# Second LayerNorm by scaling the first one's turned rows, and MLP chunks in the order 2, 3, 0, 1

## The chip, the cores and the metric

The kernel runs on one core of one Trainium2 chip. The metric is the time of one execution on the device in microseconds (us), as a median of several runs; lower is better.

## What is computed

A transformer block on 2048 tokens of 448 features in float32: a grouped-key attention (16 heads of 28, one key and one value head) and an MLP of 1792 hidden features, both on a normalized input, added to the input. The MLP normalizes a second time:

```python
def _layernorm(x, axis=-1, eps=1e-5):
    m = jnp.mean(x, axis=axis, keepdims=True)
    v = jnp.var(x, axis=axis, keepdims=True)
    return (x - m) / jnp.sqrt(v + eps)

xn = _layernorm(x)
def B(x):                      # the MLP
    y = _layernorm(x)          # the second LayerNorm
    h = gelu_tanh(y @ w1 + b1)
    return h @ w2 + b2
return x + attention(xn) + B(xn)
```

The second LayerNorm of a row has mean zero to start with, so it only multiplies the first one's row by a factor that belongs to the token: 1 / sqrt(v / (v + eps) + eps).

## The kernel before, in words

The 2048 tokens are 16 tiles of 128 tokens, four tiles make a chunk, and there are four chunks. Three stages follow each other.

**QKV.** For each chunk c and each of four column groups i there is a slot (c, i). `q_slot` (line 350) multiplies the turned rows of the chunk with the q, k and v weights; `evac` (360) brings the product from PSUM to SBUF in the next slot and sends q to DRAM (`qd`, 377). While chunk c is multiplied, chunk c + 1 is normalized: `center` (255) computes (x - mean) * rstd for a tile of 128 tokens, ScalarE for 448 columns (263) and VectorE for 64 of them once more (264); `turn` (268) transposes it on TensorE in four 128x128 blocks (272), ScalarE copies the result from PSUM as the high part `xh` (273), and VectorE subtracts for the low part `xl` (274). High and low parts are the two addends in which every factor of a float32 product is kept; a product is three matmuls (high-high, low-high, high-low), in `proj_steps` (175). Features 384 to 447 stand twice in the fourth block, so that it needs only two matmuls. The tiles `xh` and `xl` have two buffers each. During the last chunk, chunk 0 is normalized again with the second norm's factors (`norm_parts` with `second`, called at 447). The factors `lnq` and offsets `lnqb` are made by `norm_both` (231) in slots (2, 2) and (2, 3).

Between the matmuls of the stage the weights of the MLP are loaded and split: `w1_load` and `w1_load2` (315, 320; `pair` is one buffer), `w1_split` (325: ScalarE high, GpSimd low), `w2_load` (332). A dictionary of jobs (`later`, 406) puts small jobs into a given slot. All DMAs of this stage but six are issued by SyncE, in the order of the program: x, weights, the stores `qd<-qe` (377) and `ks<-kl` (374), and the loads of query tiles `qm` and `q3` (`load_m`, 433).

**MLP.** 56 slots, one for each chunk c and each of 14 groups ft of 128 hidden features, in the order of c then ft. `slot` (643) issues `mlp1` (596): 11 matmuls of the first layer into the PSUM tile `ph`, then GELU on ScalarE and GpSimd (lines 603 to 618); and `mlp2` (622) of the slot two before: 12 matmuls of the second layer into four PSUM tiles that are kept for a whole chunk. After each matmul the generator yields, and the main loop (697) puts 9 matmuls of another kind into each slot: score matmuls of the attention (`max_stream`, 511, with a maximum on VectorE at 522, and `turned_scores`, 549, with a scaled copy on VectorE at 556). All of these use the same three PSUM tiles `m`. The twelve places in `mlp2` carry jobs (`stages`): two exponentials of turned scores on ScalarE with their stores to DRAM (`turned_exp`, 568), the second half of w2's split (`low` in `w2_split`, 344, in odd slots of the first chunk), `closing` (high and low part of the GELU, 613), `middle` (tanh and the products after it, 608). In five of fourteen slots of the first three chunks the table `norms` (674) puts `norm_gen` (303) there: it centres and turns the tiles of the next chunk with the second norm's factors, using x rows that `line` (245) has loaded again.

**Attention.** From about 479 us on; the change touches nothing in it.

The order on every engine is the order of the program text (`manual_schedule`); GpSimd, VectorE, ScalarE, TensorE and SyncE's DMA queue each work in order.

Of the kernel before, what the change touches and what calls it, by code (L numbers as in the profile page):

```python
# [16 lines left out]
P = 128  # L17
# [16 lines left out]
LEAD = 11  # L34
NH = 8
# [4 lines left out]
def block_kernel(ctx, tc, x, wq, wk, wv, wo, w1, b1, w2, b2, out):  # L40
# [22 lines left out]
    td = {u: dram.tile([32, 4, 4 * CT, 512], F32, name=f"td{u}") for u in TURNED}  # L63
    qd = [dram.tile([D, S], F32, name=f"qd{i}") for i in range(2)]
# [12 lines left out]
    lnqb = wp.tile([P, NT], F32, name="lnqb")  # L77
# [171 lines left out]
    def norm_parts(c, second, first=False, bank=mtile):  # L249
        xh = xt_p.tile([P, 4, CW], F32R, name="xh")  # L250
        xl = xl_p.tile([P, 4, CW], F32R, name="xl")
        xts[c, second] = xh, xl
        xns = {}

        def center(k):
            t = CT * c + k
            if first:
                xn = f(wqp.tile([P, 2, CW], F32R, name="qe", bufs=5))[:, 0, :]
            else:
                xn = tmp.tile([P, 4 * P], F32, name="xn", bufs=2)  # L260
            scale, bias = (lnq, lnqb) if second else (lnr, lnb)
            src = lines.pop(t) if second and c else xin[t]
            act.activation(xn[:, 0:D], src, AF.Identity, bias=bias[:, t:t + 1], scale=scale[:, t:t + 1])
# [14 lines left out]
    def norm_first(bank):  # L278
        center, turn = norm_parts(0, False, True, bank)
# [72 lines left out]
    def q_slot(c, i):  # L352
        xh, xl = xts[c, False]
# [62 lines left out]
    for k in (2, 3):  # L416
        later(2, k, lambda g=g: next(g))

# [27 lines left out]
    for c in range(NCH):  # L446
        center, turn = norm_parts((c + 1) % NCH, c + 1 == NCH, bank=lambda shape: (qbank, mtile)[next(turns) % 2](shape))
        for i in range(4):
# [22 lines left out]
            for part, k in (("", "c0 c1", "t0 c2 t1 c3", "t2 t3") if c == 0 else  # L471
                            ("c0 c1", "t0 c2 t1 c3", "t2 t3", ""))[i].split():
                (center if part == "c" else turn)(int(k))
# [122 lines left out]
    def mlp1(c, ft):  # L596
        yh, yl = xts[c, True]
# [24 lines left out]
    def mlp2(c, ft, stages):  # L622
# [8 lines left out]
        for n, (k, i) in enumerate(order):  # L631
# [3 lines left out]
            if ft == NF - 1 and i == 2:  # L635
                t = CT * c + k
# [6 lines left out]
    def slot(n):  # L643
# [17 lines left out]
        if n in norms:  # L661
            stages = {4: norms[n], 5: texp, 6: texp, 7: closing, 8: norms[n], 9: middle, 10: low}
# [9 lines left out]
    norms, maxed, ending, later_low = {}, 0, none, none  # L672
    mslots = [(c, ft) for c in range(NCH) for ft in range(NF)]
    for c in range(1, NCH):
        g = norm_gen(c, lambda shape: php.tile(shape, F32, name="ph"))
        for i in range(CT + 1):
            norms[NF * (c - 1) + 5 + 2 * i] = lambda g=g: next(g, None)
    mxs.add(max_stream())
    done = 0
    for n in range(len(mslots) + 2):  # L680
        c, ft = mslots[n] if n < len(mslots) else (NCH, n - len(mslots))
        if 3 <= ft < 11 and ft % 2 and c < NCH - 1:
            line(CT * (c + 1) + (ft - 3) // 2)
        if 9 < ft:
            line(CT * c + ft - 10)
            if ft > 10:
                a = lines[CT * c + ft - 11]
                pool.tensor_add(a, a, b2b)
        if ft == 0 and n:
            a = lines[CT * c - 1]  # L690
# [263 lines left out]
```

## Time and profile before

| | us |
|---|---|
| median of 3 runs (lowest to highest) | 1092.6 (1092.5 to 1093.32) |
| profiled execution | 1092.67 |
| its span in the trace | 1090.9 |
| QKV stage, to the first MLP matmul | 66.2 |
| MLP stage | about 412 |
| attention | about 612 |

In the rows of the trace a line like `start us, us, engine, line, operation, out<-in xcount` is one instruction or a run of equal ones. PE is TensorE, DVE is VectorE, ACT is ScalarE, POOL is GpSimd and SP is SyncE. A bracket at the end tells how long the engine was idle before it and what ended that. Groups of instructions have their count, busy time and the mean of one in ns. In rows of stretches the columns are the stretch, its length, each engine's busy time with a count, the granted clock of TensorE, the busy share of the DMA engines and GB/s. Lines are those of the kernel before.

### The profile page before, as it was taken

The numbers are of one execution on the slowest core, as the hardware profiler recorded it, in microseconds if no ns is written. First come the engines' busy times: TensorE is split into PE (matmuls) and PEld (weight loads), VectorE is DVE, ScalarE is ACT, GpSimd is POOL, SyncE is SP. The second block draws the span as 40 slices with busy tenths as digits, with TensorE's granted clock in tenths as the row PEclk, the third lists the DMA queues.
The fourth block names the chain that finished last, engine by engine and source line by source line (L and its number), as shares of the span: only waits on it lengthen the run. The fifth ranks groups of instructions, "written<-read, shape, count | busy, mean of one in ns | idle before, by whom it ended". The sixth has DMA issues, their size and how long they took to land.

```text
span 1090.9 us, 17542 instructions
## 1 busy us (share of the span) xinstructions
PE 1079.5 (99%) x5777; PEld 713.7 (65%) x5777; DVE 910.4 (83%) x1847; ACT 736.4 (68%) x1279; POOL 562.5 (52%) x694
## 2 busy tenths in 40 slices
PE   9999999999999999999999999999999999999998
PEld 8778888888888888865555556555556455555444
DVE  7789889888988998887898997899986889876744
ACT  6675565666666666559777776677775777765783
POOL 6359787778767877854343433433342343243220
PEclk9999999999999999999999999999999999999999
DMA  8774555777877777767977799588797778895720
GB/s 274 214 231 136 154 145 157 194 176 185 217 181 180 183 201 180 214 161 156 200 189 175 183 212 214 141 198 193 183 202 183 175 172 194 203 197 137 183 46 35
DMA packets 140512, 195.15 MB, mean 179 GB/s; under 512 B 17086, under 2 KB 96116, under 8 KB 140420
## 3 DMA queue, kind: packets, MB, share of 16 engines
q1 hardware_dynamic: 127684, 172.11, 63.0%
q0 software_dynamic: 11328, 21.33, 8.9%
q8 instruction: 46, 0.75, 0.3%
q10 hardware_dynamic: 1408, 0.57, 0.2%
q14 instruction: 46, 0.38, 0.1%
HBM read 115.22 MB, written 77.71 MB: 177 GB/s over the span
## 4 chain that ended last, share of the span: by engine, by line
PE 89%; ACT 3%; DVE 3%; DMA 2%; POOL 1%; issue 1%; SPq 0%; DVEq 0%; ACTq 0%; POOLq 0%
PE po L840 22%; PE m L521 17%; PE m L871 17%; PE m L633 10%; PE ph L180 9%; PE m L555 5%; PE qp L180 1%; DMA td<-raw 1%; PE m L752 1%; DVE mx L522 1%; PE m L753 1%; PE m L754 1%; PE ph L185 1%; PE ph L183 1%; ACT raw L573 1%; PE m L399 1%
## 5 line engine op out<-in xcount | busy, mean ns | idle before, releaser
L522 DVE TENSOR_REDUCE mx<-m 128x1 f32<-128x512 f32 x784 | 506.5, 680 | 81.1 <-PE m L521 72.3
L872 ACT ACTIVATE p<-m 128x512 f32<-128x512 f32 x784 | 402.6, 609 | 163.2 <-PE m L871 163.2
L521 PE MATMUL m<-ks,qm 128*128 128x512 f32 x784 | 322.1, 411 | 0.1
L871 PE MATMUL m<-xh,ks 128*128 128x512 f32 x784 | 258.6, 399 | 1.0 <-DVE half L723 1.0
L840 PE MATMUL po<-p,vs 128*32 128x512 f32 x2048 | 246.0, 598 | 0.0
L521 PEld LDWEIGHTS m<-ks,qm 128*128 128x128 f32 x784 | 147.0, 187 | 117.9 <-ACT p L872 34.5
L871 PEld LDWEIGHTS m<-xh,ks 128*128 128x128 f32 x784 | 144.2, 188 | 52.0 <-ACT p L872 15.0
L556 DVE TENSOR_SCALAR_CACHE_REDUCE raw<-m 128x512 f32<-128x512 f32 x240 | 161.1, 689 | 15.2 <-PE m L555 7.0
L854 DVE STREAM_TRANSPOSE p<-half 128x1024 f32<-128x1024 f32 x120 | 148.2, 1236 | 5.3 <-PE po L840 3.3
L573 ACT ACTIVATE raw<-raw,m 128x1024 f32<-128x1024 f32 x120 | 133.1, 1151 | 0.0
L840 PEld LDWEIGHTS po<-p,vs 128*32 128x32 f32 x2048 | 53.5, 109 | 120.1 <-issue 114.2
L603 ACT ACTIVATE hx<-ph,b1t 128x512 f32<-128x512 f32 x55 | 37.9, 690 | 131.9 <-PE ph L185 122.1
L555 PE MATMUL m<-ks,q 128*128 128x512 f32 x240 | 94.8, 395 | 1.1 <-DVE mx L522 0.6
L618 POOL TENSOR_TENSOR hl<-hx,hh 128x512 fp32r<-128x512 f32 x56 | 73.2, 1306 | 34.6 <-ACT hh L616 34.6
L633 PE MATMUL m<-w2h,hl 128*128 128x448 f32 x224 | 82.5, 370 | 0.3 <-POOL hl L618 0.3
L633 PE MATMUL m<-w2l,hh 128*128 128x448 f32 x224 | 81.4, 365 | 0.4 <-DVE w2l L346 0.4
L633 PE MATMUL m<-w2h,hh 128*128 128x448 f32 x224 | 81.4, 364 | 0.1
L611 POOL TENSOR_TENSOR hx<-hx,hz 128x512 f32<-128x512 f32 x56 | 73.1, 1306 | 4.7
L606 POOL TENSOR_TENSOR hz<-hz,hx 128x512 f32<-128x512 f32 x56 | 72.8, 1299 | 4.7
L508 POOL DMA_DIRECT2D xh<-mn x15 | 8.1, 543 | 124.3 <-ACT mn L504 124.3
L180 PE MATMUL ph<-xh,w1h 128*128 128x512 f32 x165 | 65.0, 394 | 0.0
L180 PE MATMUL ph<-xh,w1l 128*128 128x512 f32 x165 | 64.6, 391 | 0.0
(181 smaller groups left out, 1376.0 us busy)
## 6 DMA issues: line engine op xcount, KB each, us to landing
td<-raw SPq DMA_DIRECT2D x240, 256.0 KB
half<-td SPq DMA_DIRECT2D x120, 512.0 KB
xh<-qd POOLq DMA_DIRECT2D x60, 168.0 KB, 4.6
a<-in_A_x_dram SPq DMA_DIRECT2D x32, 224.0 KB
qm<-qd POOLq DMA_DIRECT2D x112, 56.0 KB, 4.4
qd<-qe SPq DMA_DIRECT2D x24, 256.0 KB
qm<-qd SPq DMA_DIRECT2D x84, 56.0 KB
ad<-a SPq DMA_DIRECT2D x16, 224.0 KB
```

What stands on the lines that cost most here:

```text
L180: pe.matmul(ps, w, v, start=(n == 0), stop=False)
L521: pe.matmul(pm, qm[:, t * P:(t + 1) * P], ks[:, n * CW:(n + 1) * CW], start=True, stop=True)
L522: dve.tensor_reduce(mx[:, CT * j + t, n:n + 1], pm, axis=AX.X, op=ALU.max)
L555: pe.matmul(sc, q3[i][:, t * P:(t + 1) * P], ks[:, n * CW:(n + 1) * CW], start=True, stop=True)
L556: dve.tensor_scalar(raw[:, :, 4 * n:4 * n + 4, :].rearrange("p r b i -> p b r i"), sc.rearrange("p (b r i) -> p b r i", r=4, i=32), SCALE, ...
L573: act.activation(raw[:, rs], raw[:, rs], AF.Exp, bias=m3[:, 4:5], scale=1.0)
L618: pool.tensor_sub(hl, hx, f(hh))
L633: pe.matmul(m2[k], h[:, k * P:(k + 1) * P], w[:, ft, :], start=(ft == 0 and i == 0), stop=(ft == NF - 1 and i == 2))
L840: pe.matmul(po[32 * j:32 * j + 32, :], vs[:, kt, :], ps.pop((u, kt, j)), start=(kt == 0), stop=(kt == NT - 1))
L854: dve.transpose(p.rearrange("p k (g j) -> p g k j", j=32), halves[u, kt // 8][:, :, 32 * (kt % 8):32 * (kt % 8) + 64].rearrange("p g (k j) ...
L871: pe.matmul(s, ks[:, kt * P:(kt + 1) * P], qss[u][:, j, :], start=True, stop=True)
L872: act.activation(p, s, AF.Exp, scale=SCALE)
```

## The change

The second norm no longer starts from x. The turned rows of the first norm are taken, high and low part are added again (`join`), multiplied with a tile that holds the factors of the chunk's 512 tokens in every partition (`scaled`), and split again (`high` on ScalarE, `low` on VectorE), block by block of 128 features. The factors are transposed once on TensorE (`scale_rows`), written to DRAM, and read back as a broadcast row for each chunk (`scale_load`). Chunks 2 and 3 are still in SBUF at the end of QKV and are scaled in place; chunks 0 and 1 are joined during QKV by GpSimd, stored to DRAM (`put`) and read back in the MLP (`take`). So the MLP takes the chunks in the order 2, 3, 0, 1. Chunk 2 is scaled in the last two QKV slots, with products on VectorE; the others in the MLP, with products on GpSimd, and for chunk 3 the join on VectorE. `norm_both` runs one slot earlier, and the centred tiles of the first norm are kept in the GELU's buffers `hz`.

```diff
+MLP_ORDER = 2, 3, 0, 1
...
+    xd = [dram.tile([P, 4, CW], F32, name=f"xd{c}") for c in range(2)]
+    sd = dram.tile([NCH, CW], F32, name="sd")
...
-        dve.tensor_mul(lnq, lnq, lnr)
-        dve.scalar_tensor_tensor(lnqb, lnp[:, :, 0], -1.0, lnq, op0=ALU.mult, op1=ALU.mult)
...
-                xn = tmp.tile([P, 4 * P], F32, name="xn", bufs=2)
-            scale, bias = (lnq, lnqb) if second else (lnr, lnb)
-            src = lines.pop(t) if second and c else xin[t]
+                xn = hrp.tile([P, CW], F32, name="hz", bufs=2)
+            scale, bias, src = lnr, lnb, xin[t]
...
-    def norm_gen(c, bank):
-        center, turn = norm_parts(c, True, False, bank)
-        for k in range(CT + 1):
-            if k > 0:
-                turn(k - 1)
-            yield
-            if k < CT:
-                center(k)
-            yield
+    scales, parts = {}, {}
+
+    def scale_rows():
+        pa = mtile([NT, P])
+        pe.transpose(pa, lnq, ident)
+        at = part_tile()[0:NT, 0:P]
+        dve.tensor_copy(at, pa)
+        nc.sync.dma_start(sd.rearrange("c (k p) -> (c k) p", p=P), at)
+
+    def scale_load(c):
+        scales[c] = tmp.tile([P, CW], F32, name="ab", bufs=1)
+        nc.sync.dma_start(scales[c], sd[c:c + 1, :].to_broadcast([P, CW]))
+
+    def part_tile():
+        return tmp.tile([P, CW], F32, name="part", bufs=1)
+
+    def join(c, b, eng, part):
+        xh, xl = xts[c]
+        parts[c, b] = part
+        eng.tensor_add(part, f(xh[:, b, :]), f(xl[:, b, :]))
+
+    def put(c, b):
+        n = P if b < 3 else 64
+        nc.sync.dma_start(xd[c][0:n, b, :], parts.pop((c, b))[0:n])
+
+    def take(c, b):
+        n = P if b < 3 else 64
+        parts[c, b] = part_tile()
+        for r in range(0, P, n):
+            nc.sync.dma_start(parts[c, b][r:r + n], xd[c][0:n, b, :])
+
+    def scaled(c, b, eng):
+        eng.tensor_mul(parts[c, b], parts[c, b], scales[c])
+
+    def high(c, b):
+        if c < 2 and b == 0:
+            xts[c] = xt_p.tile([P, 4, CW], F32R, name="xh"), xl_p.tile([P, 4, CW], F32R, name="xl")
+        act.activation(xts[c][0][:, b, :], parts[c, b], AF.Copy)
+
+    def low(c, b):
+        yh, yl = xts[c]
+        dve.tensor_sub(yl[:, b, :], parts.pop((c, b)), f(yh[:, b, :]))
...
-    for k in (2, 3):
+    for k in (1, 2):
         later(2, k, lambda g=g: next(g))
+    later(2, 3, scale_rows)
+    later(2, 3, lambda: scale_load(2))
+    for c in range(3):
+        for b in range(4):
+            name = "hz" if c == 2 and b > 1 else "hx"
+            later(c, b, lambda c=c, b=b, name=name: join(c, b, pool, hrp.tile([P, CW], F32, name=name, bufs=2)))
+            if c < 2:
+                later(c + (b + 1) // 4, (b + 1) % 4, lambda c=c, b=b: put(c, b))
+    for b in range(4):
+        later(3, 2, lambda b=b: scaled(2, b, dve), b < 2)
+        later(3, 2, lambda b=b: high(2, b), b < 2)
+    for b in range(4):
+        later(3, 2 + b // 2, lambda b=b: low(2, b), b > 1)
...
-        if n in norms:
-            stages = {4: norms[n], 5: texp, 6: texp, 7: closing, 8: norms[n], 9: middle, 10: low}
+        stages.update(seconds.pop(n, {}))
...
+    for i, c in enumerate(MLP_ORDER[1:]):
+        for b in range(4):
+            n = NF * i + 4 + 2 * b
+            seconds[n] = {11: lambda c=c, b=b: scaled(c, b, pool)}
+            if c > 1:
+                seconds[n][6] = lambda c=c, b=b: join(c, b, dve, part_tile())
+            seconds[n + 1] = {7: lambda c=c, b=b: high(c, b), 11: lambda c=c, b=b: low(c, b)}
...
-        if 3 <= ft < 11 and ft % 2 and c < NCH - 1:
-            line(CT * (c + 1) + (ft - 3) // 2)
+        if ft == 1 and c < NCH - 1:
+            scale_load(MLP_ORDER[c + 1])
+        if 4 <= ft < 12 and ft % 2 == 0 and c < NCH - 1 and MLP_ORDER[c + 1] < 2:
+            take(MLP_ORDER[c + 1], ft // 2 - 2)
```

What is left out renames tiles by `MLP_ORDER[c]` where it was c, drops the fourth call of `norm_parts` in QKV, and drops `lnqb`.

More of the change, by code (lines that the diff above doesn't have):

```diff
@@ L247, in line, with norm_parts @@
         nc.sync.dma_start(lines[t], xv[:, t, :])
-    def norm_parts(c, second, first=False, bank=mtile):
+    def norm_parts(c, first=False, bank=mtile):
         xh = xt_p.tile([P, 4, CW], F32R, name="xh")
         xl = xl_p.tile([P, 4, CW], F32R, name="xl")
-        xts[c, second] = xh, xl
+        xts[c] = xh, xl
         xns = {}
@@ L352, in q_slot @@
     def q_slot(c, i):
[L353 removed]
+        xh, xl = xts[c]
         cols = slice(c * CW, (c + 1) * CW)
@@ L670, in none @@
         pass
-    norms, maxed, ending, later_low = {}, 0, none, none
+    maxed, ending, later_low = 0, none, none
     mslots = [(c, ft) for c in range(NCH) for ft in range(NF)]
[L674 to L677, printed above, removed]
+    seconds = {}
+    for i, c in enumerate(MLP_ORDER[1:]):
[5 more added lines that the diff above has]
+            seconds[n + 1] = {7: lambda c=c, b=b: high(c, b), 11: lambda c=c, b=b: low(c, b)}
     mxs.add(max_stream())
```

18 lines of the change are left out of this document (9 added, 9 removed).

## Prediction

> **What bounds the kernel now.** I read the page first, then TensorE's rows in order of time, and then the queues that must feed the changed part: SyncE's DMA issues, VectorE, ScalarE and GpSimd around one MLP slot.
>
> ```profile
> span 1090.9 us, 17542 instructions
> ...
> PE 89%; ACT 3%; DVE 3%; DMA 2%; POOL 1%; issue 1%; SPq 0%; DVEq 0%; ACTq 0%; POOLq 0%
> ```
>
> The chain is TensorE for 89%. The profiled execution took 1092.67 us (1.8 us beside its span), the median is 1092.6, so a difference in the trace is a difference of the median. A measurement of this kernel can tell about 0.2%, 2.2 us, from no change.
>
> The changed part lies in the QKV stage (to 66.24 us) and the MLP (56 slots, to about 479). In the MLP TensorE streams with no gap. The last first-layer matmul (L185) of a slot shows the slot's length; here those of slots 6, 7 and 8, and of 21 and 22:
>
> ```profile
> 106.63 0.39 PE L185 MATMUL ph<-xl,w1h 128*128 128x512 f32 x1
> 113.66 0.39 PE L185 MATMUL ph<-xl,w1h 128*128 128x512 f32 x1
> 121.77 0.39 PE L185 MATMUL ph<-xl,w1h 128*128 128x512 f32 x1
> ...
> 216.24 0.39 PE L185 MATMUL ph<-xl,w1h 128*128 128x512 f32 x1
> 223.87 0.39 PE L185 MATMUL ph<-xl,w1h 128*128 128x512 f32 x1
> ```
>
> A plain slot is 7.03 us. One that turns a tile for the second norm is 7.63, or 8.11 where VectorE also splits w2. Three turns have the 8.11 and nine about 7.63. So the second norm costs the MLP 3 x 1.08 + 9 x 0.60 = 8.6 us now.
>
> **What goes.** All 64 transposes of the second norm: 48 in the MLP, worth those 8.6 us, and 16 in the last QKV chunk:
>
> ```profile
> 58.58 0.60 PE L272 MATMUL qp<-ident,xn 128*128 128x128 f32 x4
> 59.02 0.60 PE L272 MATMUL m<-ident,xn 128*128 128x128 f32 x4
> ...
> 62.43 0.65 PE L272 MATMUL qp<-ident,xn 128*128 128x128 f32 x4
> 63.21 0.66 PE L272 MATMUL m<-ident,xn 128*128 128x128 f32 x4
> ...
> 66.47 0.39 PE L180 MATMUL ph<-xl,w1h 128*128 128x512 f32 x1
> ```
>
> They hold TensorE from 58.58 to 59.37 and from 62.43 to 63.63, 2.0 us. The one new transpose (the factors, 16x128) costs as much as a quarter of a row of four, 0.1. By itself this would end QKV 1.9 us earlier. The x rows that were read again for three chunks are replaced by as many bytes (eight parts of 256 KB and four broadcasts). I cost that exchange at nothing: the DMA share in the MLP (last column but one) leaves room, and a part has a whole slot until GpSimd wants it. If a part came later than that, GpSimd's product and what follows it would be late by the same.
>
> ```profile
> 66.24:478.70 412.46, 409.36 (x1859) 341.63 (x1858) 369.63 (x811) 253.88 (x357) 320.21 (x308) 1.00 0.68 177
> ```
>
> Also gone are ScalarE's and VectorE's halves of the second norm, 16 times centring and 16 times splitting a turned tile:
>
> ```profile
> L263 ACT ACTIVATE xn<-a,lnqb,lnq 128x448 f32<-128x448 f32 x12 | 9.0, 752 | 0.0
> L274 DVE TENSOR_TENSOR xl<-ph,xh 128x512 fp32r<-128x512 f32 x12 | 8.3, 692 | 11.3 <-ACT xh L273 11.3
> ```
>
> I count nothing for them: they stand beside TensorE's stream, and the slots of 8.11, where they don't, are counted already. The statistics of the second norm move one QKV slot ahead (some 1 us of small VectorE work in front of evictions); the wait found below covers that.
>
> **What comes in the MLP.** Twelve subtractions ("low") on VectorE, each behind a ScalarE copy ("high"), which stands behind the slot's tanh; twelve products on GpSimd; four sums ("join") on VectorE. GpSimd has room for its products: it is busy for 320 of the 412 us above, and twelve at L618's 1.3 are 16. The low does not fit. One slot begins at 198.96:
>
> ```profile
> 198.87 0.62 ACT L616 ACTIVATE hh<-hx 128x512 fp32r<-128x512 f32 x1
> 199.39 0.62 ACT L609 ACTIVATE hz<-hz 128x512 f32<-128x512 f32 x1
> ```
> ```profile
> 199.57 1.30 POOL L618 TENSOR_TENSOR hl<-hx,hh 128x512 fp32r<-128x512 f32 x1 [0.58 <-ACT hh L616]
> ```
> ```profile
> 199.70 0.69 DVE L556 TENSOR_SCALAR_CACHE_REDUCE raw<-m 128x512 f32<-128x512 f32 x1
> ```
> ```profile
> 201.72 0.39 PE L555 MATMUL m<-ks,q 128*128 128x512 f32 x1
> ```
>
> VectorE reaches the low when it would take the L556 of 199.70. But the high starts behind the tanh (L609), 0.52 later as these two follow each other, and takes 0.62 like L616: 199.91 to 200.53. Then GpSimd's L618 runs until 200.87. A VectorE subtraction of two SBUF tiles does not run beside a GpSimd tensor operation, as the w2 splits show:
>
> ```profile
> 164.03 0.65 DVE L346 TENSOR_TENSOR w2l<-raw,w2h 128x448 fp32r<-128x448 f32 x1
> ```
> ```profile
> 86.67 1.48 DVE L346 TENSOR_TENSOR w2l<-raw,w2h 128x448 fp32r<-128x448 f32 x1
> ```
> ```profile
> 86.37 1.30 POOL L611 TENSOR_TENSOR hx<-hx,hz 128x512 f32<-128x512 f32 x1
> ```
>
> The slow one started 1.0 us before L611's end and waited it out. So the low works from 200.87 to about 201.4. The delayed L556 frees its PSUM bank at 201.4 + 0.69 = 202.1. The scores have three banks; the fourth score matmul is the one of 201.72, and it waits 0.4 us. A low costs 0.45 with the hiccup behind a stall. Without the port wait it would be 0.2, and where it meets a w2 split, 0.75. I take 0.45. Slot 15, where four adds of 0.61 delay VectorE, shows the mechanism:
>
> ```profile
> 179.75 0.68 DVE L556 TENSOR_SCALAR_CACHE_REDUCE raw<-m 128x512 f32<-128x512 f32 x1
> ```
> ```profile
> 180.50 0.50 PE L555 MATMUL m<-ks,q 128*128 128x512 f32 x1
> ```
>
> The first bank was free at 179.75 + 0.68 = 180.43, and the fourth score starts at 180.50, 0.07 behind that. Sum: 12 x 0.45 + 4 joins x 0.1 = 5.8. **MLP: 8.6 + 0.3 (one more stall at a transpose) - 5.8 = 3.1 us gained**, bounds 0 and 6.
>
> **What comes in QKV, and decides.** Chunk 2 is now first in the MLP, and its rows must be multiplied by the broadcast factors first. These go to DRAM and back, issued by SyncE behind the loads of the second q3 tile. SyncE runs late:
>
> ```profile
> 39.33 1.85 SPq L438 DMA_DIRECT2D qm<-qd  x4
> ```
> ```profile
> 43.23 0.44 SPq L100 DMA_DIRECT2D pair<-in_B_w_dram  x1
> ```
> ```profile
> 60.01 2.91 SPq L438 DMA_DIRECT2D q<-qd  x4
> ```
>
> The q<-qd loads are issued two slots ahead of the transposes of 58.58 in the program, but leave after them, until 62.9. So the factors' write leaves at 62.9 at the earliest, however early VectorE has them. The same pattern is in the trace, a small write to DRAM and its broadcast back:
>
> ```profile
> tr<-ld POOLq DMA_DIRECT2D x56, 64.0 KB, 3.6
> ```
> ```profile
> ld<-rc POOLq DMA_DIRECT2D x14, 8.0 KB, 3.9
> ```
>
> That is 3.9 + 3.6 = 7.5 us (bounds 4 and 11, as these are of GpSimd's queue at another time), and SyncE stands still for the first part. The factors are there at 70.4 if nothing else is late.
>
> The Trainium skill (page "DMA: Bandwidth & Descriptors", section "Anatomy of one DMA") has a fixed cost of about 2.0 us and 436 GB/s above it for a transfer from another queue, which would be an estimate of 4.6 us for the two. By it the sum below would be 2.9 us less.
>
> More is late. SyncE must also issue eight new stores ("put"). GpSimd's joins share two buffers with them, so a join waits for the store two before it to land, and w1's splits wait behind that join:
>
> ```profile
> 39.44 1.65 POOL L329 TENSOR_TENSOR w1l<-pair,w1h 128x672 fp32r<-128x672 f32 x1 [2.65 <-ACT w1h L328]
> 41.17 0.67 POOL L330 TENSOR_TENSOR w1h<-pair,w1h 64x224 fp32r<-64x224 f32 x1
> ```
> ```profile
> SPq L377 <- DMA pair<-in_B_w_dram: 3.5, 2, 2.2
> ```
>
> This split (the fourth) releases the load of 43.23. In the new order join (1,2) stands ahead of it and waits for put (1,0). SyncE issues that behind the qm loads, at 41.2, and by the 3.6 above it lands at 44.8; join 1.3 and split 2.3 make 48.4, so the load leaves 5.2 us later and SyncE stands idle before it. It gets back up to 2.2, its longest wait for the landing of such a load, as the queue has drained meanwhile. The factors' write leaves 3.0 late, at 65.9 (bounds 0, if the stores land at once, and 8, if the other stores and joins add theirs in full). The factors land at 73.4.
>
> Then VectorE does four products and the first low, 5 x 0.65 = 3.2, before TensorE's second MLP matmul: 76.6, where it is 66.47 now, +10.1. Behind them stand two more lows and two PSUM evictions ahead of the first score bank, so the fourth score of slot 0 waits too: +1 (0 to 2). **QKV: 11.1 us lost**, the 2 us of transposes being swallowed by the wait. TensorE's queue is in order; nothing behind can fill it. The attention is not touched: its work is the same and comes later.
>
> **Sum:** 11.1 - 3.1 = +8.0 us; 1092.6 + 8.0 = 1100.6. Own range 1095 (no store delays) to 1106.
>
> **Rivals.**
> *The factors come in time* (faster). Place: the write and broadcast of the factors. If they land by 62, TensorE goes from QKV into the MLP 2.0 us earlier than now: 1092.6 - 2.0 - 3.1 = 1087.5. It turns at a landing near 66.3, where the loss equals the 3.1 of the MLP. For it: the factors are worked out a slot earlier than they were. Against: the 62.9 of SyncE, which nothing in the change advances. 0.14.
> *About even:* no store delays (write at 62.9) and lows near 0.2, a gain of 5.8 in the MLP; with 7.5 for the two transfers that is 11.1 - 3.0 - 5.8 = +2.3, and a microsecond less for them, as SyncE's may be quicker than GpSimd's, puts it inside 2.2. 0.08.
> *The joins hold the turns.* The turned tiles have two buffers, so chunk 2's turns wait for join (0,3), chunk 3's for join (1,3), which wait for stores. By my times they are let go about 1 us late; if each store lands 3 us later, TensorE waits in both chunks and the chain above moves by some 5: 1105.6. 0.15.
> *A cold TensorE.* At the start of the trace the same 128x128 matmuls come at 20 in 4.0 us, and then 23 in 2.4:
>
> ```profile
> 1.70:5.70 4.00, 4.00 (x20) 4.00 (x20) 1.00 0.99 281
> 5.80:8.20 2.40, 2.40 (x23) 2.40 (x22) 1.00 1.09 374
> ```
>
> That is 0.20 against 0.104, so the first 20 lost 1.9 us. If the wait before the MLP brings this back, 1102.5. The Trainium skill ("TensorE: Matmul & The Clock Gate", "What's actually happening") says an idle window of about 3.4 us halves the clock until one such window was busy. The trace agrees for the start; no stretch of it is idle that long later, so it can't show the rest. Slot 0 waits for VectorE as well, which would hide part. 0.12.
>
> **How the numbers follow.** Forecast 0.51, with the two slower rivals 0.78 slower by over 0.2%; same 0.08; faster 0.14. Range 1092 to 1108: from the edge of "even" to the joins' case with 2.4 us for a later store.
>
> **What would show it.** TensorE idle for about 10 us before the first MLP matmul, released by ScalarE's high or VectorE's low, and these by the broadcast; SyncE's factor write near 66; no L272 after the third chunk; MLP slots of 7.03 throughout, but for about 7.5 with a low. I am wrong if the broadcast lands before 66, if lows cost over 0.7, or if the gap before the MLP is there and the end comes no later.

## The result and the profile after

The changed kernel takes 1113.17 us as a median (1112.05 to 1115.53, five runs), the kernel before 1092.6 us (1092.31 to 1093.32, five runs): the ratio is 1.0188, 95% interval 1.0177 to 1.02. The forecast was 1100.6 us, in a range of 1092 to 1108. The profiled execution took 1112.07 us, 19.4 us more than that of before.

Two rows of TensorE's timeline cut that difference into stages: the last first-layer matmul of MLP slot 1 and that of slot 55 (columns: start, duration, engine, line, operation). It is L185 before and L187 after. First before, then after.

```profile
72.85 0.39 PE L185 MATMUL m<-xl,w1h 128*128 128x512 f32 x1
461.83 0.39 PE L185 MATMUL ph<-xl,w1h 128*128 128x512 f32 x1
```
```profile
87.51 0.40 PE L187 MATMUL m<-xl,w1h 128*128 128x512 f32 x1
481.55 0.39 PE L187 MATMUL ph<-xl,w1h 128*128 128x512 f32 x1
```

| stage | before | after | difference | forecast |
|---|---|---|---|---|
| to the end of MLP slot 1 | 72.85 | 87.51 | +14.7 | +11.1 |
| MLP slots 2 to 55 | 388.98 | 394.04 | +5.1 | -3.1 |
| from there to the end of the span | 629.07 | 628.55 | -0.5 | 0 |

The rest, 0.2 us, lies outside the span. So both stages came out worse than forecast, and the MLP with the other sign.

**QKV.** SyncE's timeline after shows the two dependent transfers: the write of the factors, and the broadcast load that waits for it.

```profile
66.13 1.83 SPq L483 DMA_DIRECT2D q<-qd  x4
68.06 0.31 SPq L309 DMA_DIRECT2D sd<-part  x1
72.01 0.34 SPq L313 DMA_DIRECT2D ab<-sd  x1
```

The write leaves right behind the query loads, at 68.06, where 65.9 was forecast. VectorE's timeline shows the load's end, four products and the first of the subtractions:

```profile
75.68 1.29 DVE L334 TENSOR_TENSOR hx<-hx,ab 128x512 f32<-128x512 f32 x2 [5.07 <-DMA ab<-sd]
76.89 1.28 DVE L334 TENSOR_TENSOR hz<-hz,ab 128x512 f32<-128x512 f32 x2
78.10 1.28 DVE L343 TENSOR_TENSOR xl<-hx,xh 128x512 fp32r<-128x512 f32 x2
```

From 68.06 to 75.68 are 7.6 us (7.5 were forecast). TensorE's first and second MLP matmul wait for what comes of it; the bracket is the idle time and what ended it:

```profile
77.09 0.80 PE L182 MATMUL ph<-xh,w1h 128*128 128x512 f32 x1 [4.93 <-ACT xh L339]
78.83 0.80 PE L182 MATMUL ph<-xl,w1h 128*128 128x512 f32 x1 [0.95 <-DVE xl L343]
```

The second is at 78.83; it was at 66.47 before. TensorE's own stream is late too. Its waits from 20 to 84 us, grouped by what it waited for (us in total, times, longest):

```profile
PE ph L182 <- ACT xh L339: 4.9, 1, 4.9
PE qp L271 <- ACT hz L262: 3.6, 4, 2.1
PE m L306 <- DVE lnq L203: 1.9, 1, 1.9
PE ph L182 <- DVE xl L343: 0.9, 1, 0.9
PE m L271 <- DVE hz L263: 0.9, 1, 0.9
```

The L271 rows are the turns of chunks 2 and 3 that wait for their centred tiles (5.5 us with two smaller groups that are not shown), and L306 is the factors' transposition. The longest wait, 2.1 us, is ahead of chunk 3's turns. Before the centring VectorE works out chunk 3's statistics, on four columns. Two of these steps take 1.26 and 1.52 us where the two ahead of them (at 46.01 and 46.21) take 0.16 and 0.17, and each ends with an instruction of GpSimd, first a join and then a split of w1. First VectorE, then GpSimd:

```profile
46.41 1.26 DVE L203 SCALAR_TENSOR_TENSOR lnr<-rs 128x4 f32<-128x4 f32 x1
47.70 1.52 DVE L222 SCALAR_TENSOR_TENSOR lnb<-lnp,lnr 128x4 f32<-128x4 f32 x1
```
```profile
46.33 1.32 POOL L321 TENSOR_TENSOR hx<-xh,xl 128x512 f32<-128x512 f32 x1 [4.21 <-DMA xd<-hx]
47.60 1.60 POOL L361 TENSOR_TENSOR w1l<-pair,w1h 128x672 fp32r<-128x672 f32 x1
```

By its bracket the join had itself waited 4.21 us for a store to land.

**MLP.** A plain slot is longer than before: from 205.81 to 212.89 are 7.08 us.

```profile
205.81 0.39 PE L185 MATMUL ph<-xh,w1h 128*128 128x512 f32 x1
212.89 0.39 PE L185 MATMUL ph<-xh,w1h 128*128 128x512 f32 x1
```

The mean over long stretches is 7.07, before it was 7.03. And the slot behind a low of chunk 3 is 8.2 to 8.3 us, behind the last of the four 9.3. Behind the lows of chunks 0 and 1 it is 7.51, behind the last of each four 8.57. Here is one of chunk 3, first ScalarE, then VectorE, then TensorE:

```profile
118.83 0.63 ACT L655 ACTIVATE hz<-hz 128x512 f32<-128x512 f32 x1 [1.81 <-POOL hz L652]
119.37 0.62 ACT L339 ACTIVATE xh<-part 128x512 fp32r<-128x512 f32 x1
```
```profile
120.09 1.62 DVE L343 TENSOR_TENSOR xl<-part,xh 128x512 fp32r<-128x512 f32 x1 [0.75 <-ACT xh L339]
```
```profile
122.38 0.51 PE L601 MATMUL m<-ks,q 128*128 128x512 f32 x1 [0.86 <-DVE raw L602]
```

The rounding (L339, "high") stands behind the tanh (L655), and the tanh waits for GpSimd, whose chain carries the product with the factors and a w2 split as well. So VectorE stands still at its subtraction (L343, "low"), 0.75 us by this row, with the score evictions behind it, and TensorE's score waits for a bank. All twelve lows together:

```profile
L343 DVE TENSOR_TENSOR xl<-part,xh 128x512 fp32r<-128x512 f32 x12 | 13.4, 1114 | 13.5 <-ACT xh L339 10.1 <-POOL hl L664 3.4
```

VectorE was busy with them for 13.4 us and idle ahead of them for 13.5.

### The profile page after: what moved, and what is told of

It is laid out like the page before. It is cut to its first block, busy times and chain, and to the rows that moved or that the text cites. A ratio compares the mean times of both kernels' runs of the same rounds, so it can differ in the third digit from the quotient of the medians.

```text
span 1110.1 us, 17459 instructions
## 1 busy us (share of the span) xinstructions
PE 1079.5 (97%) x5714; PEld 708.6 (64%) x5714; DVE 922.7 (83%) x1838; ACT 726.0 (65%) x1263; POOL 596.7 (54%) x718
## 4 chain that ended last, share of the span: by engine, by line
PE 80%; ACT 5%; DVE 4%; DMA 4%; issue 2%; POOL 2%; SPq 2%; DVEq 0%; ACTq 0%; POOLq 0%
PE po L891 21%; PE m L922 17%; PE m L567 17%; PE m L679 9%; PE ph L182 7%; PE m L601 4%; DMA td<-raw 2%; ACT raw L619 2%; PE m L803 1%; SPq L483 1%; PE m L804 1%; PE m L805 1%; DVE raw L602 1%; PE ph L187 1%; PE ph L185 1%
## 5 line engine op out<-in xcount | busy, mean ns | idle before, releaser
L568 DVE TENSOR_REDUCE mx<-m 128x1 f32<-128x512 f32 x784 | 502.8, 678 | 79.1 <-PE m L567 74.6
L182 PE MATMUL ph<-xh,w1h 128*128 128x512 f32 x165 | 65.9, 400 | 4.9 <-ACT xh L339 4.9
L182 PE MATMUL ph<-xl,w1h 128*128 128x512 f32 x165 | 66.3, 402 | 0.9 <-DVE xl L343 0.9
```

The source lines that it names most:

```text
L182: pe.matmul(ps, w, v, start=(n == 0), stop=False)
L568: dve.tensor_reduce(mx[:, CT * j + t, n:n + 1], pm, axis=AX.X, op=ALU.max)
```

## The experiments

The theory after these rows: four separate losses, (1) the factors' way through SyncE and DRAM, (2) joins and stores that hold SyncE and the turns, (3) the low's wait for the high, (4) the longer plain slot. Rivals: a cold TensorE, and VectorE having no room for the lows at all. "Slot 1 ends" is the time of the row shown above for each kernel's profiled execution. In some of these executions a single MLP slot had a stall of some 1.5 us more, which moves a single profile, not the medians. The kernel before ran beside each set of experiments, with medians of 1092.97 to 1093.3 us, and the ratios are against those; by the ratios the gains over the changed kernel come out up to 0.8 us larger than by the times.

| kernel | time (lowest to highest) | ratio to before, interval | slot 1 ends | slots 2 to 55 |
|---|---|---|---|---|
| before | 1092.6 | | 72.85 | 388.98 |
| changed | 1113.17 (1112.05-1115.53) | 1.0188, 1.0177-1.02 | 87.51 | 394.04 |
| a1_place | 1112.78 (1111.93-1115.9) | 1.0184, 1.0169-1.0199 | 89.25 | 395.94 |
| a2_no_puts | 1106.53 (1105.55-1108.47) | 1.0124, 1.0109-1.0139 | 81.24 | 394.00 |
| a3_known_factors | 1109.03 (1108.93-1110.24) | 1.0147, 1.0132-1.0162 | 83.28 | 394.29 |
| a4_high_early | 1106.01 (1105.48-1107.07) | 1.0115, 1.0098-1.0132 | 89.11 | 387.28 |
| b1_warm | 1121.13 (1116.45-1123.4) | 1.0239, 1.022-1.0258 | 97.22 | 395.61 |
| b2_joins_only | 1108.98 (1108.37-1112.44) | 1.0148, 1.0134-1.0162 | 84.77 | 396.91 |
| b3_before_w1_moved | 1095.86 (1095.62-1097.74) | 1.0027, 1.0018-1.0036 | 73.31 | 391.49 |
| b4_early_factors | 1100.26 (1099.44-1103.48) | 1.0068, 1.0054-1.0081 | 85.66 | 383.96 |
| c1_two_chunks | 1096.38 (1095.95-1097.59) | 1.0033, 1.002-1.0045 | 80.17 | 385.11 |
| c2_stores_by_gpsimd | 1101.25 (1100.01-1101.73) | 1.0073, 1.0059-1.0086 | 86.29 | 384.41 |
| d1_two_chunks_order | 1093.5 (1093.19-1094.59) | 1.0006, 0.9997-1.0014 | 76.61 | 386.09 |
| d2_all_order | 1098.1 (1097.56-1098.62) | 1.0046, 1.003-1.0061 | 84.46 | 383.71 |
| e1_products_shared | 1093.48 (1092.33-1094.91) | 1.0005, 0.9996-1.0014 | 76.73 | 386.40 |
| e2_lows_later | 1094.72 (1092.73-1095.83) | 1.0012, 1.0003-1.0021 | 77.57 | 386.32 |

### The longer plain slot: where the weights lie

The change removes the 64-byte tile `lnqb`, and all that is allocated behind it moves down by 64 bytes. In a1 an unused tile takes its place; in b3 the kernel *before* gets the same shift for w1h and w1l (and three small tiles) alone.

```diff
+    gap = wp.tile([P, NT], F32, name="gap")
     b1t = wp.tile([P, NF], F32, name="b1t")
```
```diff
-    lnqb = wp.tile([P, NT], F32, name="lnqb")
     b1t = wp.tile([P, NF], F32, name="b1t")
...
     w1l = wp.tile([P, 3, F], F32R, name="w1l")
+    lnqb = wp.tile([P, NT], F32, name="lnqb")
```

> The changed kernel with one more small tile of 64 bytes a partition, never used, in the place of the removed one, so that the weights w1h and w1l, the tiles of hrp and w2h and w2l lie at the addresses they had before. If the slower plain MLP slot (7.07 us instead of 7.03 us) comes from where the operands lie, a plain slot is 7.03 us again and the kernel takes 2.3 us less (55 slots x 0.041): about 1110.9 us. If it comes from the order of the instructions or from the engines beside TensorE, the slot stays at 7.07 us and the time at 1113.2 us.

> The kernel before, with its 64-byte tile lnqb allocated behind w1l instead of ahead of b1t, so that w1h and w1l alone lie 64 bytes lower, as in the changed kernel, and nothing else differs. If the place of w1 makes a plain slot 7.07 us, this kernel takes 2.3 us more than before: 1094.9 us. If it is the place of w2h, w2l or the tiles of hrp, or no matter of places, it takes as long as before: 1092.6 to 1093.3 us.

Two neighbouring slot ends in a1, and two in b3:

```profile
209.15 0.39 PE L186 MATMUL ph<-xh,w1h 128*128 128x512 f32 x1
216.18 0.39 PE L186 MATMUL ph<-xh,w1h 128*128 128x512 f32 x1
```
```profile
196.68 0.40 PE L185 MATMUL ph<-xl,w1h 128*128 128x512 f32 x1
203.78 0.40 PE L185 MATMUL ph<-xl,w1h 128*128 128x512 f32 x1
```

In a1 a plain slot is 7.03 us again; in b3 it is 7.07 to 7.11 us. The time of a1 doesn't settle it (0.4 us less where 2.3 were expected; its interval is 3 us wide, and the profiled execution, the longest of its four, had two of the stalls named above), but b3's does: 2.9 us more than before (interval 2.0 to 3.9) from moving tiles by 64 bytes, with the order of the instructions unchanged. In the trace it is a few ns on a matmul: from 270 to 300 us the means of the first layer's groups are 389 to 394 ns before and 393 to 399 ns in b3. Why these addresses are slower, no run here shows.

### Factors, joins and stores

a2 leaves out joins and stores of chunks 0 and 1 (first diff), b2 the stores alone (second diff, with the same loads of w1's rows in the MLP). a3 reads chunk 2's "factors" from a row of w1, early (third diff).

```diff
-    for c in range(3):
+    for c in range(2, 3):
         for b in range(4):
...
-            nc.sync.dma_start(parts[c, b][r:r + n], xd[c][0:n, b, :])
+            nc.sync.dma_start(parts[c, b][r:r + n], w1[0:n, 320 * b:320 * b + CW])
```
```diff
-            if c < 2:
-                later(c + (b + 1) // 4, (b + 1) % 4, lambda c=c, b=b: put(c, b))
```
```diff
-    later(2, 3, lambda: scale_load(2))
+    def known(c):
+        scales[c] = tmp.tile([P, CW], F32, name="ab", bufs=1)
+        nc.sync.dma_start(scales[c], w1[c:c + 1, 0:CW].to_broadcast([P, CW]))
+
+    later(2, 0, lambda: known(2))
```

> Leaves out the joins and the stores to DRAM of chunks 0 and 1; the loads in the MLP read rows of w1 instead, so chunks 0 and 1 of the MLP work on other numbers at the same cost. If the stores hold SyncE and the joins hold the turns (TensorE waits of 1.17 us at 33.08 and 2.22 us at 50.13, the pair load of w1 at 49.97 instead of 43.23), the QKV part ends 3 to 5 us earlier, the factors' write leaves SyncE at 63 to 65 instead of 68.06, and the kernel takes 3 to 5 us less: about 1109. If the write is late for its own reasons (the wait of 2.09 us for lnq ahead of the transposition at 60.85, the queue's other loads), less than 1 us is gained: 1112 to 1113.

> Leaves out the stores of chunks 0 and 1 to DRAM, but keeps GpSimd's joins (the MLP's loads read rows of w1 again, so chunks 0 and 1 work on other numbers). Without joins and stores the kernel took 1106.5 us. If the stores are what delays QKV, through SyncE's queue, this takes 1106.5 to 1108 us. If it is the joins, which hold xh and xl and VectorE's small operations (one of the 16-column steps of lnq took 0.17 us or up to 1.5 us), it stays at 1111 to 1113 us.

> Chunk 2's factors are read from a row of w1 early in its slot 0 instead of from the stored factors, so that nothing waits for the write and the load behind it; chunk 2 is scaled by wrong numbers, all instructions stay. If the two transfers make the wait between QKV and MLP and that idle time makes TensorE cold, the second MLP matmul follows the last QKV matmul (near 72) at once, slot 0 runs at full clock, and the kernel takes 6 to 8.5 us less: 1105 to 1107. If VectorE's own backlog (products and lows behind the rest of its queue) is what is late, at most 2 us is gained: 1111 or more. Without the cold clock in it, 5 us: 1108.

The write of the factors leaves SyncE at 62.19 in a2 and at 65.02 in b2, 68.06 in the changed kernel; a2's row, then b2's:

```profile
62.19 0.31 SPq L309 DMA_DIRECT2D sd<-part  x1
```
```profile
65.02 0.31 SPq L309 DMA_DIRECT2D sd<-part  x1
```

So the joins alone make the write 2.8 us later and the stores another 3.0. In time, the stores are worth 4.2 us and the joins 2.4 (1113.17, 1108.98, 1106.53). The turns' waits of 5.5 us are 1.2 us in a2. Both halves of the theory hold, neither alone: a2 was expected at about 1109 and went lower, b2 lies between its two cases.

a3 gained 4.1 us, less than the 6 to 8.5 expected, and nearest to the 5 that it gave without a cold clock: without the wait for the factors TensorE's own QKV stream, which the turns make late, is the next bound. Its first MLP matmul follows the last QKV matmul at once:

```profile
72.69 0.40 PE L187 MATMUL qp<-xl,wah 128*128 128x512 f32 x1
72.92 0.44 PE L182 MATMUL ph<-xh,w1h 128*128 128x512 f32 x1
74.61 0.50 PE L182 MATMUL ph<-xl,w1h 128*128 128x512 f32 x1 [1.24 <-DVE xl L343]
```

**The cold TensorE** did come. Two stretches of slots 0 and 1 of the changed kernel (the figure after the five busy times is the granted clock):

```profile
79.40:83.24 3.84, 3.84 (x10) 3.01 (x9) 3.84 (x5) 1.25 (x2) 2.82 (x2) 0.50 0.69 253
84.00:87.05 3.05, 3.05 (x15) 2.49 (x14) 3.02 (x10) 2.37 (x4) 1.35 (x2) 1.00 0.23 86
```

By a3 it cost nothing. From the second MLP matmul to the end of slot 1 the changed kernel takes 87.51 - 78.83 = 8.68 us; a3, which is not cold (a granted clock of 1.00 from 74.6 to 83.3), takes 83.28 - 74.61 = 8.67 us. a3 waits for VectorE instead: its third and fourth low and the evictions behind them set the end. Before, the same stretch took 72.85 - 66.47 = 6.38 us.

b1 was to test this by idle matmuls that keep TensorE busy:

```diff
     evac()
+    spin(50, mtile([P, P]))
     ph1a.close()
```

> The changed kernel with 50 idle matmuls of 128 columns (0.09 us each by the transposes' rows, 4.5 us) between the last QKV matmul and the MLP, so that TensorE does not stand idle while the factors come. If slot 0's slow matmuls (0.43 us instead of 0.23 us) cost the 2.2 us that slot 0 is longer by, the kernel takes about 2 us less: 1111. If the next wait takes their place (with the factors known early slot 0 ended 6.25 us earlier but slot 1 waited 1.95 us more), less than 0.5 us is gained: 1112.7 to 1113.2. In an execution whose QKV stream ends only at 77 the idle matmuls come on top, up to 4 us.

The experiment missed. The 50 matmuls left 100 records and held TensorE from 79.39 to 90.47, 11.1 us instead of the 4.5 expected, and QKV ended late in this execution anyway (the wait for `lnq` was 5.3 us, not 1.9). It says nothing on the cold clock; a3 against the changed kernel does.

### The low waits for the high

```diff
-            seconds[n + 1] = {7: lambda c=c, b=b: high(c, b), 11: lambda c=c, b=b: low(c, b)}
+            seconds[n + 1] = {4: lambda c=c, b=b: high(c, b), 11: lambda c=c, b=b: low(c, b)}
```

> The second norm's rounding on ScalarE goes from stage 7 to stage 4 of its slot, ahead of the tanh that waits for GpSimd; nothing else changes. If VectorE's wait for that rounding (0.75 to 1.1 us for each of chunk 3's four lows, 2.27 us for the last of chunks 0 and 1) is what the MLP loses, that goes and the kernel takes 5 to 8 us less: 1105 to 1108. If the lows cost because VectorE has no room for 0.7 to 1.6 us more of work, the stalls of TensorE stay at 1.0 us a low in chunk 3's stage and the time within 1 us: 1112 to 1113.

One digit, and 7.2 us: 1106.01. The same slot as above on ScalarE, now with the rounding ahead of the tanh, and the slot behind the low on TensorE:

```profile
118.49 0.63 ACT L339 ACTIVATE xh<-part 128x512 fp32r<-128x512 f32 x1
120.42 0.63 ACT L655 ACTIVATE hz<-hz 128x512 f32<-128x512 f32 x1 [1.29 <-POOL hz L652]
```
```profile
116.10 0.39 PE L185 MATMUL ph<-xh,w1h 128*128 128x512 f32 x1
123.17 0.40 PE L185 MATMUL ph<-xh,w1h 128*128 128x512 f32 x1
```

The slot of 8.2 us is 7.07 us long. VectorE's group of the lows after that edit:

```profile
L343 DVE TENSOR_TENSOR xl<-part,xh 128x512 fp32r<-128x512 f32 x12 | 16.8, 1396 | 3.1 <-ACT xh L339 2.7 <-DMA q<-qd 0.4
```

The idle time ahead of the lows fell from 13.5 to 3.1 us, though each got longer (1396 ns; it now begins while GpSimd works). So it was the wait; the rival that VectorE has no room falls for chunk 3's lows. In the other two stages the lows of blocks 0 to 2 still cost the 0.44 us of before the edit, slots of 7.51 against 7.07, and the last ones 0.9 (slots of 8.0) instead of 1.5.

### The mends together, and a version with two chunks

b4 joins the unused tile, the early high, and chunk 2's factors worked out early from its own four tiles. c2 is b4 with the stores issued by GpSimd. c1 keeps the factors for chunks 2 and 3 alone and turns chunks 0 and 1 in the MLP as before, without their joins and stores; its transposition of chunk 2's factors is one slot later than in b4. d1 and d2 are c1 and b4 with another order of chunk 2's steps. e1 and e2 take work of d1 from VectorE, or move it.

In b4:

```diff
-    g = norm_both()
+    g = norm_both(8, CT)
     for k in (1, 2):
-        later(2, k, lambda g=g: next(g))
-    later(2, 3, scale_rows)
-    later(2, 3, lambda: scale_load(2))
+        later(1, k, lambda g=g: next(g))
+    later(1, 3, lambda: scale_rows(8, CT))
+    later(2, 1, lambda: scale_load(2))
+    g = norm_both()
+    for k in (2, 3):
+        later(2, k, lambda g=g: next(g))
+    later(3, 2, scale_rows)
...
     for b in range(4):
-        later(3, 2, lambda b=b: scaled(2, b, dve), b < 2)
-        later(3, 2, lambda b=b: high(2, b), b < 2)
+        later(3, b // 2, lambda b=b: scaled(2, b, dve))
+        later(3, b // 2, lambda b=b: high(2, b))
     for b in range(4):
-        later(3, 2 + b // 2, lambda b=b: low(2, b), b > 1)
+        later(3, 1 + b // 2, lambda b=b: low(2, b), True)
```

In c1, on top of b4 (`norm_gen` and its loads are those of the kernel before):

```diff
-    for c in range(3):
+    for c in range(2, 3):
         for b in range(4):
...
+    for i, c in enumerate(MLP_ORDER[2:], 1):
+        g = norm_gen(c, lambda shape: php.tile(shape, F32, name="ph"))
+        for k in range(CT + 1):
+            norms[NF * i + 5 + 2 * k] = lambda g=g: next(g, None)
-    for i, c in enumerate(MLP_ORDER[1:]):
+    for i, c in enumerate(MLP_ORDER[1:2]):
```

In c2, on top of b4, and in d1 and d2, on top of c1 and b4:

```diff
-        nc.sync.dma_start(xd[c][0:n, b, :], parts.pop((c, b))[0:n])
+        nc.gpsimd.dma_start(xd[c][0:n, b, :], parts.pop((c, b))[0:n])
```
```diff
-    later(2, 1, lambda: scale_load(2))
...
-        later(3, b // 2, lambda b=b: scaled(2, b, dve))
-        later(3, b // 2, lambda b=b: high(2, b))
-    for b in range(4):
-        later(3, 1 + b // 2, lambda b=b: low(2, b), True)
+        later(3, 0, lambda b=b: scaled(2, b, dve))
+    for b in range(4):
+        later(3, 1, lambda b=b: high(2, b))
+    for b in range(4):
+        later(3, 1, lambda b=b: low(2, b))
...
+            if (c, i) == (2, 1):
+                scale_load(2)
             if i in ((2, 3) if c == 0 else (1, 3)):
```

In e1, on top of d1, and in e2, on top of e1:

```diff
-    for b in range(4):
-        later(3, 0, lambda b=b: scaled(2, b, dve))
+    for b in (2, 0, 3, 1):
+        later(3, 0, lambda b=b: scaled(2, b, dve if b < 2 else pool))
```
```diff
-        later(3, 1, lambda b=b: low(2, b))
+        later(3, 1 + b // 2, lambda b=b: low(2, b), b > 1)
```

> All three mended at once: the unused 64-byte tile (places as before), the rounding at stage 4 in the MLP, and chunk 2's factors worked out in slots 1 and 2 of chunk 1 from its own four tiles, written in slot 3 and loaded in chunk 2's slot 1, so that chunk 2 is scaled in slots 0 to 2 of chunk 3; the other factors are written in slot 2 of chunk 3. If the three losses are separate they add up: 1113.2 - 7.2 - 2.3 - 4.1 = 1099.6 us. If the wait for the factors was the only floor under the end of QKV, it goes lower, to 1095; if the joins and stores hold TensorE's own stream, the second MLP matmul is still at 72 to 76 us and the time is 1099 to 1103 us.

> The kernel with the three mends (early factors, rounding at stage 4, places as before; 1100.3 us), with the eight stores of chunks 0 and 1 issued by GpSimd, right behind its joins, instead of by SyncE. If it is SyncE's queue (0.43 to 0.6 us for each issue, none idle between 58 and 68) that the stores lengthen, most of the 4.2 us that came back without the stores comes back here: 1096 to 1098 us. If it is the transfers themselves, or GpSimd pays for the issue with its own time ahead of the w1 splits, 1100 us or more.

> A version of both kernels: chunks 2 and 3, which stay on the chip, get their second LayerNorm by factors (chunk 2's worked out early, the rounding at stage 4, places as before), and chunks 0 and 1 by loading their rows again and turning them, as in the kernel before; no join or store of chunks 0 and 1. If joins and stores of chunks 0 and 1 are the 6.6 us that QKV still loses, QKV and slot 0 end at 71 to 73 (69.2 before, 80.9 with the three mends), chunk 3's stage of the MLP takes 2 us less than before, chunks 0 and 1's as long as before, and the kernel takes 1091 to 1094 us. If the joins of chunk 2 and the factors themselves hold QKV, slot 0 still ends at 76 to 80 and it takes 1097 to 1100 us.

> The kernel with the three mends and the stores of chunks 0 and 1 (1100.3 us), with the same order of chunk 2's steps, its factors transposed in slot 0 of chunk 2. If the order was worth 4 to 6 us, 1094 to 1096 us, and the rest to the version with two chunks, about 4 us, is the price of the joins and stores of chunks 0 and 1. If SyncE's queue sets the end of QKV, less than 2 us is gained: 1098 to 1100 us.

> The version with factors for chunks 2 and 3 alone (1096.4 us), with three steps of chunk 2 put elsewhere: the factors' load issued in chunk 2's slot 1 ahead of the loads of w2 and of the queries (at about 53 instead of 57.22), all four products on VectorE in slot 0 of chunk 3, and the four roundings on ScalarE in slot 1, behind the eviction that the values' transposition waits for. If the waits of 2.42 us (transposition of the values), 0.95 and 1.57 us (slot 0 of the MLP) come from that order alone, slot 0 ends at 69 to 71 instead of 75.1 and the kernel takes 1090 to 1092 us, less than both. If they come from VectorE's and GpSimd's load at the end of QKV, whatever the order, it takes 1094 to 1096 us.

> The version with factors for chunks 2 and 3 in the better order (1093.5 us), with two of chunk 2's four products on GpSimd, which does nothing from 59.2 to 63.3, instead of on VectorE. If VectorE's own work is what is left at the end of QKV (busy without a gap from 55 to 75; TensorE waits 1.8 us for its copy of the values and 0.6 us for its scores), 0.6 to 1.3 us is gained: 1092.2 to 1092.9 us. If SyncE's queue or the order on ScalarE is what is left, or GpSimd's products hold VectorE's by as much as they take from it, it stays within 0.4 us of 1093.5.

> As the kernel with the shared products, and chunk 2's third and fourth difference go one slot later, behind the copy of the values that TensorE's third PSUM bank waits for. If VectorE's queue is what is left, the wait of 1.8 us ahead of the scores at 70.2 goes down and the kernel takes 1 to 2.5 us less than 1093.5: 1091 to 1092.5, less than both kernels. If the differences are then late for slot 0 of the MLP (its matmuls on their rows come at about 69.5), the wait only moves and it stays at 1093 us or more.

b4 takes 1100.26 us, where adding up the three losses gave 1099.6. That the two agree is in part luck: until the end of slot 1 b4's profile is 1.9 us ahead of the changed kernel's, where a3 was 4.2 ahead, and in slots 2 to 55 b4 gains 10.1 us instead of 9.5. Its MLP slots 2 to 55 take 383.96 us, 5.0 less than before: with the two faults mended the MLP gains what it was thought to gain, and more. But its slot 1 still ends at 85.66, 12.8 us later than before, and this is all of the remaining loss. c2 gained nothing (1101.25): to move the stores to GpSimd's queue doesn't help. So either it is not SyncE's issue time that they cost, or GpSimd pays as much for issuing them; no run separates the two. c1, without joins and stores of chunks 0 and 1, is 3.9 us faster than b4, but at 1096.38 meets neither of its two cases; slots 0 and 1 came out later than expected, as the eviction that the values' transposition needs stood on ScalarE behind the highs of chunk 2. The better order gave 2.2 us in d2 and 2.9 in d1, less than the 4 to 6 of their first cases. d1 against d2 gives the price of taking chunks 0 and 1 through DRAM in mended kernels: 1098.1 - 1093.5 = 4.6 us, of which the profiled executions show 7.85 lost until the end of slot 1 and 2.4 gained in the slots behind.

d1 takes as long as the kernel before (1.0006, interval 0.9997 to 1.0014). What it gains in the MLP (386.09 against 388.98) it loses until the end of slot 1 (76.61 against 72.85). 2.4 us of these 3.8 are waits of TensorE for VectorE, 1.8 for the copy of the values and 0.6 for an eviction of scores. The place is VectorE at the end of QKV, in d1, with GpSimd beside it:

```profile
64.66 2.06 DVE L360 TENSOR_TENSOR xl<-hx,xh 128x512 fp32r<-128x512 f32 x2
66.65 3.20 DVE L360 TENSOR_TENSOR xl<-hz,xh 128x512 fp32r<-128x512 f32 x2
69.88 0.29 DVE L434 COPY vs<-m 128x128 f32<-128x128 f32 x1
```
```profile
63.46 1.63 POOL L378 TENSOR_TENSOR w1l<-pair,w1h 128x672 fp32r<-128x672 f32 x1
...
66.27 1.97 POOL L378 TENSOR_TENSOR w1l<-pair,w1h 128x672 fp32r<-128x672 f32 x1
```

Four lows need 4 x 0.68 us where nothing is beside them (78.10 in the changed kernel: two in 1.28); here they take 5.2, beside GpSimd's splits (with a second instruction of 1.0 us behind each of the two shown), and the copy of the values is behind them. The turned differences of the kernel before have one operand in PSUM. Here one of them runs in 0.69 us in the middle of a split, VectorE first:

```profile
61.53 0.69 DVE L274 TENSOR_TENSOR xl<-qp,xh 128x512 fp32r<-128x512 f32 x1
```
```profile
60.98 1.64 POOL L329 TENSOR_TENSOR w1l<-pair,w1h 128x672 fp32r<-128x672 f32 x1 [2.43 <-ACT w1h L328]
```

e1, which moves two of the four products to GpSimd, changed nothing (1093.48): the copy is at 69.99 instead of 69.88, since VectorE's other products and its small operations then waited for GpSimd's. e2 (1094.72) moved the wait to chunk 2's lows. So the rest is at VectorE and not in SyncE's queue. These rows put it down to the work on two SBUF operands that stands beside GpSimd's; no run takes GpSimd's splits away to prove it, and no order tried here beat the kernel before.

## Why the prediction was wrong

- **The two transfers** (7.5 us): right, 7.6. **The products and the first low** (3.2): right, 75.68 to 78.83 is 3.15.
- **The write of the factors leaves at 65.9** ("3.0 late"): failed in size. It left at 68.06. The 62.9 "at the earliest" was close (62.19 without joins and stores), but the delay was counted once, as one join that waits for one store. Joins and stores cost 2.8 and 3.0 us each, 5.9 in all, within the bounds of 0 and 8.
- **VectorE's backlog** (+1, 0 to 2): 8.68 - 6.38 = 2.3 us, above its bounds. QKV in all: +14.7 instead of +11.1, of which the write is 2.2 and the backlog 1.3. The idle time "of about 10 us" ahead of the first MLP matmul was 4.9, since TensorE's own stream was late as well.
- **The MLP gains 3.1 us** ("bounds 0 and 6"): failed, with the other sign, +5.1. The step that failed is the price of the lows, 12 x 0.45 = 5.4 us; by the slots behind them they cost 11.4. The 0.45 was right for the six lows that it describes (7.51 against 7.07); the other six cost 1.1 to 2.2, above the 0.7 that the prediction names as its sign of being wrong. It said that the high stands behind the tanh, and took the tanh's time from a slot in which nothing holds it. In the slots where the tanh itself waits for GpSimd, behind the product that the change adds, with a w2 split or the adding of b2, VectorE waits for the high: a4 gained 6.8 us in slots 2 to 55. The other step that failed is "MLP slots of 7.03 throughout": a removed tile moved the operands, by estimate 54 x 0.04 = 2.2 us. Together, 11.4 + 2.2 less the 8.6 + 0.3 that go make 4.7 of the 5.1.
- **The exchange of loads, costed at nothing:** right. None of GpSimd's waits in the MLP is for a part from DRAM.
- **The rivals.** The cold TensorE came and was hidden altogether behind VectorE. (In the prediction's two rows from the start of the trace the clock column reads 1.00 for the slow matmuls too, so only the times of the matmuls speak for it there; in slot 0 the column reads 0.50.) The joins did hold the turns (5.5 us of TensorE's waits, 1.2 without joins and stores). The longest of these waits came by another way than the two buffers that the prediction names: VectorE's statistics stood beside a join and a split. In the changed kernel the factors come later still; a3 shows what TensorE's late stream makes alone, 4.1 us less than the result. Factors in time for the MLP: b4 made them earlier, and 12.8 us were still lost until the end of slot 1.
- **The range** ended at 1108, since its MLP part allowed no loss. With the high ahead of the tanh alone a4 takes 1106.01, within it; with the old addresses as well, by estimate, 1113.2 - 7.2 - 2.3 = 1103.7.

## What to carry to other kernels

Follow a new instruction's input back through *every* in-order engine in the worst slot that it meets, not in a typical one: a rounding that stands behind a waiting tanh made twelve cheap subtractions cost 7 us more than with the rounding ahead of that tanh. When a change removes or adds a small tile, look at whether the operands behind it moved, and put a dummy there before judging the change. And work that leaves TensorE for VectorE and GpSimd is not free because TensorE is the bound: here both engines' operations on two SBUF tiles took turns, and the turned path, with PSUM as one operand, was as fast.

## What the runs showed of the hardware that was not expected

- **Addresses.** With w1h and w1l (and three small tiles) 64 bytes lower, the same instructions take 7.07 to 7.11 us a slot instead of 7.03, 2.9 us over the kernel (interval 2.0 to 3.9).
- **VectorE beside GpSimd, small operations too.** In a1's execution the steps of `lnq` on 16 columns took:

```profile
60.59 1.26 DVE L202 SCALAR_TENSOR_TENSOR rs<-rs 128x16 f32<-128x16 f32 x1
61.89 1.19 DVE L203 TENSOR_TENSOR rs<-rs 128x16 f32<-128x16 f32 x1
63.11 1.52 DVE L204 SCALAR_TENSOR_TENSOR lnq<-rs 128x16 f32<-128x16 f32 x1
```

  Beside them GpSimd had its joins and splits without a gap:

```profile
60.55 1.26 POOL L322 TENSOR_TENSOR hx<-xh,xl 128x512 f32<-128x512 f32 x1
61.77 1.26 POOL L322 TENSOR_TENSOR hz<-xh,xl 128x512 f32<-128x512 f32 x1
62.99 1.60 POOL L362 TENSOR_TENSOR w1l<-raw,w1h 128x672 fp32r<-128x672 f32 x1
```

  Each step ends with one of GpSimd's instructions; in the kernel before it takes 0.18 us. One input does not spare an operation: the L195 step of the kernel before, with `lnq` as its only input, takes 1.63 us at 53.03 beside a split of w1 (52.99, 1.64 us), and 0.18 in the changed kernel (L197 there). The Trainium skill ("Trainium Architecture — The Big Picture", "What this means for kernel authors") calls the two engines' shared port pair an exclusive lock, not a split of bandwidth. The rows agree: such an operation waits for the other engine's whole instruction (1.2 to 1.6 us), whatever its own size.
- **A half clock after a short idle.** In b4 TensorE waited 2.42 us for the values and then ran at 0.53 of its clock for 3.6 us:

```profile
71.72 0.43 PE L419 MATMUL m<-ident,vt 32*128 32x32 f32 x4 [2.42 <-ACT vt L404]
```
```profile
72.11:75.70 3.59, 3.59 (x11) 2.81 (x11) 3.53 (x4) 0.39 (x1) 2.61 (x2) 0.53 0.32 106
```

  In c1 a wait of 2.28 us (ahead of 65.41) was followed by the full clock, in c2 one of 1.70 us (ahead of 70.72) by 0.52 from 71.0 to 73.2. The Trainium skill ("TensorE: Matmul & The Clock Gate", "What's actually happening") asks for an idle window of about 3.4 us; here 2.42 and 1.70 us were enough, and 2.28 were not, so the length of one wait doesn't decide it alone.
